# An infini-attention and GeGLU kernel on one core: the recall's copy and sums, the first differences of x, the loads of x's words and four sums of squares change their places

## The chip, the cores and the metric

The kernel runs on one core of a Trainium2 chip. The metric is the device time of one execution in microseconds (us). A core has five engines that run side by side and are tied together by semaphores: TensorE (PE, matmuls, with its weight loads listed as PEld), VectorE (DVE), ScalarE (ACT), GpSimd (POOL) and SyncE (SP, which here only issues DMAs). Matmul results land in PSUM, in eight banks of 128 partitions by 512 fp32 columns.

## The reference

For 2048 tokens of width 576 two branches are computed from the same x and mixed by a gate per token.

```python
def _A_ref(x, wq, wk, wv, wo, beta):          # 32 heads of 18, 4 segments of 512 tokens
    q, k, v = heads of x @ wq, x @ wk, x @ wv
    phi = lambda t: jnp.where(t > 0, t + 1.0, jnp.exp(t))
    M = z = 0
    for s in range(4):
        a_dot = causal softmax attention inside the segment
        num = phi(qs) @ M
        den = phi(qs) @ z + 1e-6
        o = g * num / den + (1.0 - g) * a_dot  # g = sigmoid(beta), per head
        M = M + phi(ks).T @ vs
        z = z + sum over tokens of phi(ks)
    return concat(o) @ wo

def _B_ref(x, w_gate, w_up, w_down):           # 4608 hidden columns
    return (gelu(x @ w_gate) * (x @ w_up)) @ w_down

g = sigmoid((x * gate_w).sum(-1, keepdims=True))
return g * a + (1 - g) * b
```

Everything is fp32 in and out.

## The kernel before

**Pairs of fp16 words.** An fp32 operand is scaled by a power of two and written as two fp16 words, high and low. A product of two such operands is three fp16 matmuls (high by high, high by low, low by high). The scales come from sums of squares, which is what `squares`, `stat_qk`, `square_x` and `scale_sum` compute.

**The part ahead of the long loop.** x is cut into four chunks `s` of 512 tokens, one per segment. Each chunk goes through two stages, written out in the loop from line 797 on:

- rows (`for q in range(4)`, not for chunk 0, whose rows are computed at the start in fp32 by `first_words`): `vrows` makes 128 tokens of v in two halves, `put_rows` evicts them; `key_rows` turns phi(k) of the chunk before with five transposes on PE, `memorize` adds phi(k)ᵀv to the memory, `recall` multiplies phi(q) of the chunk before with the memory, and `put_recall` divides by the sum and writes `mo` out to DRAM;
- columns (`for j in range(9)`): `project` makes 128 columns of q or k for the chunk's 512 tokens by `chain_w`, fourteen matmuls into one bank, and `put_columns` evicts them as word pairs (`stage`, three buffers, to DRAM) and as phi (Relu and Exp on ACT, a multiply on DVE, an addition on POOL).

The recall of chunk 1 runs in the rows of chunk 2, that of chunk 2 in the rows of chunk 3, and that of chunk 3 in the last columns of chunk 3 and after them.

**put_recall, lines 546 to 567.** A recall fills two banks, `na` with heads 0 to 20 and a part of head 21, `nb` with the rest. ACT copies the 19 columns of head 21 from `na` to the tile `hd` (L551), DVE adds them to `nb` (L552), adds 1e-6 to the 32 sums into the tile `den` (L556), takes reciprocals (L559), multiplies by the gate (L560) and writes the quotients (L563), after which the banks are free. `key_rows` of the next step takes one of them (L573).

**x's words and differences.** The FFN's products are arranged with sums and differences of operands, so that fewer products are needed. `load_sums(p)` loads the fp32 words of two chunks into the tile `acc` (L355; `acc` also holds the raw weights wv, wq and wk while these are being converted), `form_sums(p, i, half)` forms difference `i` of three on DVE (L366), its high word on ACT (L368) and its low word on DVE (L370), as `half` says; `last_sum` forms a fourth. The `words` in `kept` are `acc` seen flat.

**Order.** Inside `tc.manual_schedule` each of PE, ACT, DVE and POOL runs its instructions in the order in which the program calls them. A function such as `put_recall` is often appended to the list `later` and runs, on all engines, when `finish_later` is next called. `beside_rows`, `behind_rows` and `beside_products` are the places in a row or column where other work is put: loads of the next chunk (`next_x`), the differences, and, in chunk 3, the first FFN weights with their sums of squares (`squares`, by default on DVE at L81). SP's issues are in no such list: a planner orders them by when their operands are ready in its own model, and SP then issues in that order.

**The long loop.** From line 1383 on, 72 steps make the FFN's products, with the attention of one head and the output products of the pair before between them. The first step's products take the banks V, G and U.

Of the kernel before, what the change touches and what calls it, by code (L numbers as in the profile page):

```python
# [18 lines left out]
P = 128  # L19
# [23 lines left out]
def kernel(ctx: ExitStack, tc: tile.TileContext, xs, wqk, wv, wo, wgu, wd, beta, out):  # L43
# [279 lines left out]
    def chain_w(o, w, x):  # L323

        n = 0
        for k in range(4):
            for a, b in ((0, 0), (0, 1), (1, 0)):
                pe.matmul(o, w(k, a), x[:, 4 * b + k], start=n == 0, stop=False)  # L328
                n += 1
        pe.matmul(o, w(4, 0), x[:, 8], start=False, stop=False)  # L330
        pe.matmul(o, w(4, 1), x[:, 8], start=False, stop=True)
# [26 lines left out]
    def form_sums(p, i, half):  # L358

        r, sc = sums_x[p], xsc[:, 2 * p : 2 * p + 1]  # L360
        t = kept["xt"][p] if half >= 0 else None
        k, o, a, b = ((0, (1, 1), (1, 2), (1, 1)), (2, (1, 2), (2, 2), (1, 2)), (1, (2, 2), (2, 2), (1, 1)))[i]
        if t is not None:
            hi, lo = (flat(t[:, 4 * k + j : 4 * k + j + 2]) for j in (0, 2))
        if half <= 0:
            dve.tensor_tensor(r[o], r[a], r[b], OP.subtract)  # L366
        if half == 0 or half == 2:
            act.activation(hi, r[o], AF.Copy, scale=sc)  # L368
        if half == 1:
            dve.scalar_tensor_tensor(lo, r[o], sc, hi, OP.mult, OP.subtract)  # L370
# [35 lines left out]
    with tc.tile_pool(name="prj", bufs=2, side="right", reuse_waits="tile") as pp:  # L406
# [61 lines left out]
        def project(s, j):  # L468
            w = W[j]
            i = j % 4  # L470
            pr = bank("G") if i == 0 else bank("U") if i == 3 else bank("st", 2)
            chain_w(pr, lambda k, a: w[:, a, k * P : (k + 1) * P], x16[s])
            return s, j, pr
# [72 lines left out]
        def put_recall(s, q, na, nb):  # L546
            hf, c = divmod(s, 2)
            t = 4 * c + q
            dn = pp.tile([P, H], F32, name="den", bufs=2)
            hd = pp.tile([P, MC], F32, name="hd", bufs=2)  # L550
            act.activation(hd, na[:, HS * MC : (HS + 1) * MC], AF.Copy)  # L551
            dve.tensor_tensor(nb[:, :MC], nb[:, :MC], hd, OP.add)  # L552
            o3s = [(slice(0, HS), na[:, : HS * MC].rearrange("p (h d) -> p h d", d=MC)),
# [5 lines left out]
            dve.reciprocal(rd, dn)  # L559
            dve.tensor_tensor(rd, rd, gh[:, 0], OP.mult)  # L560
# [47 lines left out]
        with tc.manual_schedule(engines=ORDERED):  # L608
# [58 lines left out]
            for qs in ((0, 1), (2, 3)):  # L667
                for k in range(0 if qs[0] else 1, KT):
# [3 lines left out]
                    if qs[0] and k == 2:  # L672
                        turns.update(of=2)
                        scale_sum(0, wst[:, 10:19])
                        turns.update(of=3)
                        later.pop(2)()
                        make_qk(0)
                        put_rows(0, 1, 1, vb[1], usc, 1.0)
                        low_x(0, 2)
                        make_qk(1, pair_high)  # L680
                        outscale(0, 0)
                        act.activation(gh[:, 1], gh[:, 0], AF.Exp, scale=-1.0)
# [27 lines left out]
            def beside_rows(s, q):  # L710
                if s == 1 and q == 0:
                    load_sums(0)
                if s == 1 and q == 2:
                    rescale(0)
                    rescale_words(0)
                if s == 2:
                    if q:
                        form_sums(0, q - 1, 1)
                    if q < 3:
                        form_sums(0, q, 0)  # L720
# [10 lines left out]
            def behind_rows(s, q):  # L731
                if s == 3:
                    if q < 3:
                        form_sums(1, q, -1)
# [7 lines left out]
            def beside_products(s, j):  # L742
# [10 lines left out]
                if s < 3:  # L753
                    next_x(s + 1, j)
                if s == 2:
# [4 lines left out]
                    if j == 3:  # L760
                        load_sums(1)
# [3 lines left out]
                if s == 3:  # L765
# [17 lines left out]
                    if j == 7:  # L783
                        squares(1, 3, 0)
                        squares(1, 0, 2)
                    if j == 8:
                        high_g(1, 1)
                        low_g(1, 1)
                        squares(1, 3, 1)
                        squares(1, 1, 2)  # L790
# [53 lines left out]
            put_columns(*done)  # L844
            recall(3, 3)
# [674 lines left out]
```

## Time and profile before

| | us |
|---|---|
| median of 3 runs (lowest to highest) | 1585.94 (1585.93 to 1586.18) |
| the profiled execution | 1585.91 |
| its span, first to last instruction | 1584.2 |
| PE busy | 1569.1 |
| POOL, ACT, DVE busy | 1199.8, 1173.6, 1141.2 |
| DMA moved | 209.00 MB |

The granted TensorE clock was 1.00 throughout. The profile has several views: the page (busy time of each engine, the chain that ended last, the costliest groups), the busy time by stage, the timeline of one engine (start, length, line, operation, and in brackets the idle time in front with what ended it), and the instructions of one line. L551 is line 551 of the kernel before.

### The profile page before, as it was taken

How to read it: one execution, taken by the hardware profiler on the slowest of the kernel's cores; microseconds unless marked ns; L12 is line 12 of the kernel's file. 1: busy time of each engine (PE TensorE's matmuls, PEld its weight loads, DVE VectorE, ACT ScalarE, POOL GpSimd, SP SyncE). 2: the span in 40 equal slices, each digit the busy share in tenths (PEclk: the TensorE clock that was granted, in tenths of full speed). 3: DMA queues.
4: the chain of work that ended last, by engine and by line, in shares of the span. 5: the costliest groups of instructions: out<-in, count | busy, mean ns of one | idle time of the engine just before them, and what ended most of it. 6: DMA issues, size and time to landing. Idle time of an engine off the chain costs nothing.

```text
span 1584.2 us, 32578 instructions
## 1 busy us (share of the span) xinstructions
PE 1569.1 (99%) x11842; PEld 925.7 (58%) x11842; DVE 1141.2 (72%) x2982; ACT 1173.6 (74%) x1989; POOL 1199.8 (76%) x1155
## 2 busy tenths in 40 slices
PE   9999999999999999999999999999999999999999
PEld 5655754555555555555555555555555555555577
DVE  6666786777777677777677777677777777776766
ACT  6665546988888887989888888878798888874310
POOL 2232657798978888887979788888879797887774
PEclk9999999999999999999999999999999999999999
DMA  6532444877799897979788987979797979746163
GB/s 244 196 109 79 148 145 88 139 133 131 128 131 139 128 141 122 145 120 152 136 136 129 130 145 123 154 117 144 120 161 133 139 130 135 132 73 143 38 143 98
DMA packets 472305, 209.00 MB, mean 132 GB/s; under 512 B 427600, under 2 KB 437072, under 8 KB 471632
## 3 DMA queue, kind: packets, MB, share of 16 engines
q1 hardware_dynamic: 472144, 206.92, 72.1%
q8 instruction: 93, 1.52, 0.4%
q14 instruction: 68, 0.56, 0.1%
HBM read 90.99 MB, written 27.26 MB: 75 GB/s over the span
## 4 chain that ended last, share of the span: by engine, by line
PE 96%; DVE 2%; ACT 1%; issue 1%; DMA 0%; POOL 0%; DVEq 0%; ACTq 0%; POOLq 0%
PE dn L1010 26%; PE U L1050 18%; PE V L1050 12%; PE G L1050 12%; PE pv L964 4%; PE U L1056 2%; PE st L328 2%; PE G L328 2%; PE dn L338 1%; PE G L1061 1%; PE V L1061 1%; PE st L914 1%; PE U L1400 1%; PE V L1056 1%; PE G L1056 1%; PE U L328 1%
## 5 line engine op out<-in xcount | busy, mean ns | idle before, releaser
L1010 PE MATMUL dn<-paird,hh 128*128 128x288 f16 x3408 | 485.8, 286 | 0.0
L944 POOL TENSOR_TENSOR ph<-pf,ph 128x512 f16<-128x512 f32 (+1 forms) x256 | 354.2, 1406 | 165.8 <-ACT ph L943 162.8
L1050 PEld LDWEIGHTS <-pairg 128*128 128x128 f16 x3024 | 274.9, 98 | 284.9 <-issue 38.2
L1010 PEld LDWEIGHTS <-hh 128*128 128x128 f16 x3456 | 337.7, 98 | 155.8 <-issue 0.2
L1018 DVE SCALAR_TENSOR_TENSOR acc<-dn,ev,acc 128x288 f32<-128x288 f32 x536 | 275.1, 514 | 65.9 <-PE dn L1010 65.3
L933 ACT ACTIVATE pf<-pf,mb,esc 128x512 f32<-128x512 f32 (+3 forms) x512 | 292.9, 642 | 7.0 <-ACT mb L930 0.4
L1050 PE MATMUL G<-x,pairg 128*128 128x512 f16 x864 | 221.8, 380 | 1.4 <-DVE stage L490 1.3
L1050 PE MATMUL U<-xt,pairg 128*128 128x512 f16 x864 | 210.0, 379 | 0.0
L309 POOL TENSOR_TENSOR pairg<-raw,pairg 128x640 f16<-128x640 f32 (+2 forms) x144 | 175.9, 1245 | 10.5 <-ACT pairg L305 10.5
L1037 POOL TENSOR_TENSOR hh<-gl,hh 128x512 f16<-128x512 f32 x144 | 164.0, 1160 | 16.4 <-ACT hh L1036 16.4
L943 ACT ACTIVATE ph<-pf 128x512 f16<-128x512 f32 (+1 forms) x256 | 172.4, 720 | 0.0
L305 ACT ACTIVATE pairg<-raw 128x640 f16<-128x640 f32 (+2 forms) x144 | 89.9, 651 | 103.8 <-POOL raw L299 53.3
L1215 DVE COPY gl<-U 128x512 f32<-128x512 f32 x72 | 49.8, 692 | 162.0 <-PE U L1050 148.8
L920 DVE CUSTOM_DVE_ANT_0 pf<-st,mask 128x512 f32<-128x512 f32 (+1 forms) x256 | 157.0, 614 | 0.0
L274 POOL TENSOR_SCALAR raw<-raw,sc 128x640 f32<-128x640 f32 x72 | 134.9, 1887 | 0.0
L1040 ACT ACTIVATE gl<-gl,sc 128x512 f32<-128x512 f32 x144 | 96.5, 715 | 41.7 <-DVE gl L1246 28.0
L1050 PE MATMUL U<-x,pairg 128*128 128x512 f16 x432 | 126.9, 378 | 0.4 <-DVE gl L1242 0.4
L920 DVE CUSTOM_DVE_ANT_0 pf<-dn,mask 128x256 f32<-128x256 f32 (+1 forms) x256 | 80.7, 353 | 59.4 <-PE dn L914 59.4
L1036 ACT ACTIVATE hh<-gl 128x512 f16<-128x512 f32 x144 | 85.7, 619 | 28.5 <-DVE gl L1032 28.3
L1050 PE MATMUL V<-xt,pairg 128*128 128x512 f16 x432 | 105.7, 381 | 0.0
L1050 PE MATMUL V<-x,pairg 128*128 128x512 f16 x432 | 104.8, 378 | 0.9 <-DVE gl L1162 0.9
L964 PEld LDWEIGHTS <-pt 128*128 128x128 f16 x2560 | 83.2, 96 | 6.3
(295 smaller groups left out, 2590.1 us busy)
## 6 DMA issues: line engine op xcount, KB each, us to landing
raw<-in_wgu_dram SPq DMA_DIRECT2D x36, 640.0 KB
rawd<-in_wd_dram SPq DMA_DIRECT2D x36, 288.0 KB
qk<-stage SPq DMA_DIRECT2D x36, 256.0 KB
qt<-qk SPq DMA_DIRECT2D x128, 72.0 KB
kt<-qk SPq DMA_DIRECT2D x128, 72.0 KB
vp<-vstage SPq DMA_DIRECT2D x16, 296.0 KB
vt<-vp SPq DMA_DIRECT2D x16, 296.0 KB
qt<-qk SPq DMA_DIRECT2D x128, 36.0 KB
```

The costliest lines, as they stand in the source:

```text
L274: pool.tensor_scalar(r, r, scl[f // 2][0][:, 0:1], None, OP.mult)
L309: pool.tensor_tensor(spot(f, *p, 1), raw_g[f][:, p[0] : p[1]], spot(f, *p, 0), OP.subtract)
L920: dve.tensor_tensor_reduce(prob[a][:, COL[qi] : COL[qi + 1]], ov, mask[:, L - (qi + 1) * P :], 1.0, -3e38, OP.add, OP.max, mx[a][:, qi : q ...
L933: act.activation(r, r, AF.Exp, bias=b[:, qi : qi + 1], scale=esc[:, 0, c : c + 1])
L943: act.activation(h[:, 0, cols], p[:, cols], AF.Copy)
L944: pool.tensor_tensor(h[:, 1, cols], p[:, cols], h[:, 0, cols], OP.subtract)
L964: pe.matmul(ov, pr[:, 10 * i + COL[qi] // P + kb], v[:, 4 * e + kb, c0 : c0 + VC], start=kb == 0 and i == 0, stop=kb == qi and i == 1)
L1010: pe.matmul(o[:, :NH], hh[:, a, q * P : (q + 1) * P], w[:, b, n * NH : (n + 1) * NH], start=i == 0, stop=i == 5)
L1018: dve.scalar_tensor_tensor(av, o[:, :NH], ev, av, OP.mult, OP.add)
L1037: pool.tensor_tensor(hh[:, 1], t, hh[:, 0], OP.subtract)
L1040: act.activation(t, o, AF.Gelu_apprx_tanh, scale=scl[f // 2][0][:, 2 + c : 3 + c])
L1050: pe.matmul(o, w[:, i, (a + k) * P : (a + k + 1) * P], x[:, b + k], start=start and n == 0, stop=n == 5, skip_group_check=True)
```

## The change

1. In `chain_w` an option issues the eight matmuls with the weights' high word first and the four with their low word behind them. It is used for the first column tile of chunk 0 alone. Its weights' high words are made by two ACT instructions in place of one.
2. The loads of x's words for both halves (four DMAs of 1 MB) are called together in the first row of chunk 1. In front of them POOL sets one column of each of the four destinations to zero.
3. The first difference of each half (`form_sums(p, 0, -1)`) moves from the rows of chunk 2, and from behind the rows of chunk 3, to column 3 of chunks 1 and 2. Its high word stays where it was.
4. In `put_recall` the copy of head 21's columns goes from ACT to DVE, and the 32 sums and their reciprocals are kept in free columns of `na`'s bank in place of the tile `den`.
5. Four sums of squares of chunk 3's last columns (two halves of `raw_g[3]`, both `raw_d`) go from DVE to ACT (`act_square`), the last of them behind the last column's eviction.

```diff
-    def chain_w(o, w, x):
-        n = 0
-        for k in range(4):
-            for a, b in ((0, 0), (0, 1), (1, 0)):
-                pe.matmul(o, w(k, a), x[:, 4 * b + k], start=n == 0, stop=False)
-                n += 1
+    def chain_w(o, w, x, low_last=False):
+        words = [(k, a, b) for k in range(4) for a, b in ((0, 0), (0, 1), (1, 0))]
+        if low_last:
+            words.sort(key=lambda i: i[1])
+        for n, (k, a, b) in enumerate(words):
+            pe.matmul(o, w(k, a), x[:, 4 * b + k], start=n == 0, stop=False)
...
-            chain_w(pr, lambda k, a: w[:, a, k * P : (k + 1) * P], x16[s])
+            chain_w(pr, lambda k, a: w[:, a, k * P : (k + 1) * P], x16[s], s == j == 0)
...
-            dn = pp.tile([P, H], F32, name="den", bufs=2)
             hd = pp.tile([P, MC], F32, name="hd", bufs=2)
-            act.activation(hd, na[:, HS * MC : (HS + 1) * MC], AF.Copy)
+            dve.tensor_copy(hd, na[:, HS * MC : (HS + 1) * MC])
             dve.tensor_tensor(nb[:, :MC], nb[:, :MC], hd, OP.add)
+            dn = na[:, 448 : 448 + H]
...
-            dve.reciprocal(rd, dn)
-            dve.tensor_tensor(rd, rd, gh[:, 0], OP.mult)
+            dve.reciprocal(dn, dn)
+            dve.tensor_tensor(rd, dn, gh[:, 0], OP.mult)
...
-                        make_qk(0)
+                        w0 = W[0] = pp.tile([P, 2, KT * P], F16, name="wp", bufs=9)
+                        for cols in (slice(0, 2 * P), slice(2 * P, KT * P)):
+                            act.activation(w0[:, 0, cols], raw_qk[:, 0, cols], AF.Copy, scale=wsc[:, 0:1])
+                        pair_low(w0, raw_qk[:, 0], wsc[:, 0:1])
...
                 if s == 1 and q == 0:
+                    pool.memset(kept["words"][:, 2 * L : 18 * L].rearrange("p (a b) -> p a b", a=4)[:, :, 0:1], 0.0)
                     load_sums(0)
+                    load_sums(1)
...
                     if q < 3:
-                        form_sums(0, q, 0)
+                        form_sums(0, q, 0 if q else 2)
...
                 if s == 3:
-                    if q < 3:
+                    if 1 <= q < 3:
                         form_sums(1, q, -1)
...
+                if s in (1, 2) and j == 3:
+                    form_sums(s - 1, 0, -1)
...
-                    if j == 3:
-                        load_sums(1)
...
                     if j == 7:
-                        squares(1, 3, 0)
-                        squares(1, 0, 2)
+                        squares(1, 3, 0, act_square)
+                        squares(1, 0, 2, act_square)
                     if j == 8:
                         high_g(1, 1)
                         low_g(1, 1)
-                        squares(1, 3, 1)
-                        squares(1, 1, 2)
+                        squares(1, 3, 1, act_square)
...
             put_columns(*done)
+            squares(1, 1, 2, act_square)
             recall(3, 3)
```

More of the change, by code (lines that the diff above doesn't have):

```diff
@@ L360, in form_sums @@
         r, sc = sums_x[p], xsc[:, 2 * p : 2 * p + 1]
-        t = kept["xt"][p] if half >= 0 else None
+        t = kept["xt"][p] if half > -1 else None
         k, o, a, b = ((0, (1, 1), (1, 2), (1, 1)), (2, (1, 2), (2, 2), (1, 2)), (1, (2, 2), (2, 2), (1, 1)))[i]
```

## The prediction

> **What bounds the kernel now.** I read the page first, then the busy time by stage, then PE's timeline wherever a stage is not full.
>
> ```profile
> span 1584.2 us, 32578 instructions
> PE 1569.1 (99%) x11842; PEld 925.7 (58%) x11842; DVE 1141.2 (72%) x2982; ACT 1173.6 (74%) x1989; POOL 1199.8 (76%) x1155
> ...
> 100.00:136.00 36.00, 31.07 (x229) 24.30 (x228) 26.96 (x55) 17.97 (x41) 7.65 (x13) 1.00 0.34 120
> 164.00:192.00 28.00, 26.26 (x211) 22.49 (x209) 20.69 (x61) 11.36 (x31) 17.53 (x20) 1.00 0.37 132
> 205.00:231.00 26.00, 23.75 (x127) 13.58 (x126) 25.13 (x53) 11.06 (x20) 13.96 (x12) 1.00 0.40 142
> 300.00:400.00 100.00, 100.00 (x812) 58.23 (x810) 74.14 (x214) 84.58 (x143) 86.37 (x82) 1.00 0.76 132
> ```
>
> The columns after the length are PE, PEld, DVE, ACT, POOL, clock, DMA share and GB/s. TensorE is the bound: in the long loop (last row) it is busy all the time at clock 1.00, and the whole span has only 1584.2 - 1569.1 = 15.1 us without it. Most of those lie ahead of the long loop, in the three first stages above (4.9, 1.7 and 2.3 us). No edit touches a matmul's size or number, so the change can only win or lose such gaps. These are the gaps, by PE's timeline:
>
> ```profile
> 26.35 2.33 PE L328 MATMUL G<-x,wp 128*128 128x512 f16 x10 [0.32 <-DVE wp L109]
> 56.22 0.30 PE L340 MATMUL dn<-wv,x 128*128 128x288 f16 x1 [0.38 <-DVE x L184]
> 60.80 0.33 PE L574 MATMUL V<-ident,phi 128*128 128x128 f32 x1 [0.28 <-POOL phi L489]
> 112.73 0.63 PE L573 MATMUL st<-ident,phi 128*128 128x128 f32 x4 [1.87 <-DVE mo L563]
> 127.73 0.63 PE L573 MATMUL st<-ident,phi 128*128 128x128 f32 x4 [1.59 <-DVE mo L563]
> 134.22 0.63 PE L573 MATMUL st<-ident,phi 128*128 128x128 f32 x4 [1.47 <-DVE mo L563]
> 171.39 0.63 PE L573 MATMUL st<-ident,phi 128*128 128x128 f32 x4 [0.58 <-ACT vstage L508]
> 190.74 0.63 PE L573 MATMUL st<-ident,phi 128*128 128x128 f32 x4 [1.16 <-DVE mo L563]
> 224.61 1.46 PE L1050 MATMUL V<-xt,pairg 128*128 128x512 f16 x6
> 227.40 1.46 PE L1050 MATMUL G<-x,pairg 128*128 128x512 f16 x6 [1.34 <-DVE stage L490]
> 229.77 1.45 PE L1050 MATMUL V<-x,pairg 128*128 128x512 f16 x6 [0.91 <-DVE gl L1162]
> 234.81 1.29 PE U L1050 x6
> ```
>
> A bracket counts from the drawn end of the last matmul, which overlaps its successor. Measured by starts, G began 2.79 us after V where a group of six takes 1.29 (last row, from the chain), so 1.50 were lost against a bracket of 1.34; the next gap is 2.37 - 1.29 = 1.08 against 0.91. I add 0.15 us to each bracket that disappears.
>
> **The rows of chunks 2 and 3 (put_recall, form_sums).** Five gaps end at key_rows (L573), which needs the PSUM bank that put_recall drains. Why that drain is late:
>
> ```profile
> 106.05 1.37 PE L542 MATMUL st<-bd,phi 128*128 128x152 f32 x10
> 107.00 2.01 DVE L366 TENSOR_TENSOR acc<-acc 128x1024 f32<-128x1024 f32 x1
> 108.93 0.45 DVE L513 SCALAR_TENSOR_TENSOR vstage<-dn,vstage 128x288 f16<-128x288 f32 x1
> 109.05 1.15 ACT L368 ACTIVATE xt<-acc,xsc 128x1024 f16<-128x1024 f32 x1 [1.99 <-DVE acc L366]
> 110.77 0.19 ACT L551 ACTIVATE hd<-st 128x19 f32<-128x19 f32 x1
> 110.99 0.19 DVE L552 TENSOR_TENSOR st<-st,hd 128x19 f32<-128x19 f32 x1 [1.61 <-ACT hd L551]
> ...
> 128.30 1.50 PE L542 MATMUL st<-bd,phi 128*128 128x152 f32 x10
> ...
> 125.12 1.87 DVE L560 TENSOR_TENSOR rden<-rden,gh 128x32 f32<-128x32 f32 x1
> 124.61 2.35 POOL L375 TENSOR_TENSOR acc<-acc 128x1024 f32<-128x1024 f32 x1
> ```
>
> The recall's matmuls end at 107.4, but hd, a copy of 19 columns, stands on ACT behind the wide L368, which waits for DVE's first difference, and behind two evictions. DVE then sits idle for ACT. From L552's start to PE's release are 112.73 - 110.99 = 1.74 us. Now the copy is DVE's own. No row has a DVE copy of this size. It lies between nothing and the 0.19 us of L552, which reads the same 19 columns of PSUM; I take 0.19, and ACT's L551 goes in exchange. With L366 gone from that place, DVE is free at 107.0, does one L513 (0.45), and from 107.5 the copy and the drain take 1.93: released at 109.4, while PE arrives at 110.9. In the last row of the chunk the recall ends at 129.8 and the drain would be over near 132, just ahead of PE's arrival at 134.22 - 1.47 = 132.75. The middle gap also holds L560's 1.87 behind POOL's 2.35; its product now takes a PSUM operand. Even if it still waited for POOL, a row in the middle has one more half of vrows than the last row's 132.75 - 129.8 = 2.95 us between the recall's end and PE's arrival. So all three gaps go: 1.87 + 1.59 + 1.47 = **4.93**.
>
> In chunk 3 the same two causes (a difference of 1.2 us taken out ahead of the first recall, no hd on ACT in the last) take away 0.58 + 1.16 = **1.74**. The last row is the tight one: rescale_words stands on DVE before the drain.
>
> The reciprocal and the product now read dn in PSUM, and L556 writes it there. Nearest are L552 and L556, which read PSUM already; unknown is only the surplus, between a gain of the 1.87's excess and a loss of some 0.1 us a drain; I take none.
>
> [...]
>
> **The moved differences.** They run at column 3 of chunks 1 and 2. Their cover:
>
> ```profile
> 92.44 0.69 DVE L161 TENSOR_REDUCE x<-dn 128x1 f32<-128x512 f32 x1 [4.30 <-PE dn L159]
> L366 DVE TENSOR_TENSOR acc<-acc x6: 1215/1276/2006, 107.0 to 179.1; 128x1024 f32<-128x1024 f32 x6
> ```
>
> L366 took 1.2 to 2.0 us (shortest, median, longest in the row, in ns); in chunk 1 an idle time of 4.3 us stands behind it, and chunk 2 runs the same columns. Cost nothing; uncovered, one would cost its 1.2 to 2.0 us.
>
> **The words of x.** All four loads of 1 MB now wait for a memset of four columns on POOL, in chunk 1's first row, at about 60.8 us.
>
> ```profile
> 34.31 0.33 SPq L355 DMA_DIRECT2D acc<-in_xs_dram  x1
> 51.67 5.59 DMA qk<-stage
> 57.37 0.60 ACT L478 ACTIVATE stage<-G 128x512 f16<-128x512 f32 x1 [1.29 <-DMA qk<-stage]
> 50.00:61.00 11.00, 10.34 (x69) 6.45 (x67) 9.61 (x14) 7.47 (x16) 5.33 (x9) 1.00 0.90 333
> 61.00:82.00 21.00, 21.00 (x154) 16.18 (x153) 7.67 (x23) 8.93 (x23) 2.05 (x7) 1.00 0.23 84
> ```
>
> Those loads (the first of four is shown) filled the DMA engines while the column stages were written out, so ACT waited 1.29 us for a stage buffer, POOL's phi was late by it, and PE lost the **0.28** at 60.80. That goes. The four megabytes now fall into a stretch that moved 84 GB/s: at 333 GB/s 4.2 MB take 12.6 us and the stretch's own 1.8 MB another 5.3, so all is there near 79, ahead of the idle stretch of DVE (88.1 to 92.4) that could still take the first difference. The memset itself lies between nothing and the 2.35 us of a POOL instruction over 1024 columns; I take nothing, since POOL was busy 2 of 21 us there.
>
> **The first column.**
>
> ```profile
> 24.55 0.83 ACT L106 ACTIVATE wp<-acc,wsc 128x640 f16<-128x640 f32 x1 [2.36 <-DVE wsc L93]
> 25.41 0.89 DVE L109 SCALAR_TENSOR_TENSOR wp<-acc,wsc,wp 128x640 f16<-128x640 f32 x1 [0.35 <-ACT wp L106]
> ```
>
> With the high words first, PE no longer waits 0.32 for L109. But two ACT instructions cost one fixed part more (between nothing and 0.2 us; I take 0.12), L109 and all of DVE behind it move by that, the next column waits for its own low word on the same DVE queue, and the 0.38 at 56.22 hangs on DVE and ACT, not on PE. What PE gains it waits for later. I put **0**, between a gain of 0.5 and a loss of 0.2.
>
> **The end of the projections.**
>
> ```profile
> L81 DVE CUSTOM_DVE_ANT_0 junk<-raw x5: 810/1410/1807, 168.9 to 220.9; 128x640 bf16<-128x640 f32 x5
> L81 DVE CUSTOM_DVE_ANT_0 junk<-rawd x2: 1344/1465/1586, 214.8 to 222.8; 128x576 bf16<-128x576 f32 x2
> 167.23 0.72 ACT L437 ACTIVATE krow<-raw 128x640 bf16<-128x640 f32 x1
> 223.60 0.60 ACT L478 ACTIVATE stage<-G 128x512 f16<-128x512 f32 x1 [0.58 <-PE G L331]
> ```
>
> DVE was 25.1 of 26 us busy there, and PE's first FFN products waited for its queue. Four sums of squares leave it (two of 640 columns and two of 576: 2 x 1.41 + 2 x 1.47 = 5.8 us); the four copies return 0.8. ACT has them for about 0.7 us each and was busy 11 of 26 us; the last one stands behind L478, the eviction that PE's G bank needs. L478 ends at 224.2, L490, as wide, can follow by 224.8, ahead of 224.61 + 1.29 = 225.9, when V's group ends. Behind it the last drain takes until 224.8 + 1.93 = 226.7 and L1162, as wide again, until 227.4 or so, where PE wants V at 225.9 + 1.29 = 227.2. Of 1.34 + 0.91 = 2.25 I keep 0.35 as a new wait: **1.9**.
>
> **Sum.** 4.93 + 1.74 + 0.28 + 1.9 = 8.85, plus 0.15 for most of the eight gaps (five counted, since small waits on the transposes' eviction will come back as rows close up), 0.75: 9.6 us. The profiled execution took 1585.91 us, its span and 1.7 around it, beside a median of 1585.94. **1585.9 - 9.6 = 1576.3.**
>
> **Rivals.** (1) DVE becomes the bound of the rows: it now carries the copy, the drain, a difference and a low word each row, by my sum 1.93 + 2 x 0.45 + 1.2 + 1.2 = 5.2 us, where PE takes (127.73 - 1.59 - 112.73) / 2 = 6.7; were the chain late in every second row, 3.3 us would be given back: 1579.6. Against it, the drain starts at the recall's end. (2) The end is not won: ACT's squares are placed ahead of the last eviction, and G is freed 0.7 to 1.4 us late; 1.9 go and up to 0.7 more: 1578.2 to 1579. (3) Slower: SP issues in order. If the loads of words are put ahead of the stage writes of column 5 and later, all of those sit behind a wait for the memset at 60.8, three stage buffers run out, and ACT's L478 at 57.37 waits until 60.8 plus the 5.59 us that such a write took. That is about 9 us for this column and 3 more for each column earlier: 1585 for one, 1588 for two, slower than before from the second on, so from where the first load stands two writes ahead. Before, SP's order followed readiness, which speaks against it. (4) No change: the loop gives the time back. Its PE is full at clock 1.00, so only a late POOL or load at its start could do that: 1584. (5) The memset holds no load back: 0.28 less, inside the range.
>
> **How the numbers follow.** Forecast 0.66, (1) 0.15, (2) 0.08, (4) 0.06, (3) 0.05. Low end: 8.92 + 0.28 and 1.2 by starts, with the first column's 0.7, 11.1 us: 1574.8. The high end takes in (1), (2) and the unknown costs: 1581.0. What this kernel can tell from no change is about 0.2%, 3.2 us: faster 0.89, same 0.06, slower 0.05.
>
> **What would show it.** Right: no gap ahead of L573; the drain on DVE begins at the recall's end; no ACT instruction of 19 columns; the L355 issues after 60 us and the first L366 before 92 without a wait; L490 of the last column ahead of 225. Wrong: L366 waiting for a DMA, SP's stage writes queued behind L355, DVE without idle time in the rows, or PE gaps past 230 us that were not there.

## The result and the profile after

| | before | after |
|---|---|---|
| median of 4 runs each (lowest to highest), us | 1585.99 (1585.93 to 1586.18) | 1576.43 (1576.23 to 1576.74) |
| the profiled execution, us | 1585.91 | 1576.48 |
| span, us | 1584.2 | 1574.8 |

The ratio of the times is 0.994, with a 95% interval of 0.9922 to 0.9957. The kernel became 9.6 us faster, and the prediction was 1576.3.

The page of the kernel after, its first lines, and then the busy time by stage (length, PE, PEld, DVE, ACT, POOL, clock, DMA share, GB/s) for the rows of chunk 2 and the end of the projections:

```profile
span 1574.8 us, 32583 instructions
PE 1568.7 (100%) x11842; PEld 926.2 (59%) x11842; DVE 1138.9 (72%) x2986; ACT 1175.2 (75%) x1986; POOL 1196.1 (76%) x1156
...
100.00:131.00 31.00, 30.83 (x230) 24.39 (x229) 26.92 (x57) 17.84 (x38) 7.92 (x13) 1.00 0.41 145
200.00:222.00 22.00, 22.00 (x121) 12.92 (x120) 19.57 (x48) 12.11 (x22) 11.86 (x12) 1.00 0.44 150
```

PE's busy time is what it was (1568.7 against 1569.1), and the span without PE shrank from 15.1 to 6.1 us. The two stages shown had 4.9 and 2.3 us of idle PE (36 and 26 us long then) and have 0.17 and 0. So nothing became cheaper on PE; waits went away.

A bracket counts from drawn ends, so the account is made from the starts of the same matmuls in both traces. PE's timeline, first of before (rows that the prediction doesn't have), then of after:

```profile
20.23 3.20 PE L533 MATMUL st<-acc,raw 128*128 128x290 f32 x12
62.44 0.29 PE L340 MATMUL dn<-wv,x 128*128 128x290 f16 x1
105.80 0.29 PE L340 MATMUL dn<-wv,x 128*128 128x288 f16 x1
165.75 0.29 PE L340 MATMUL dn<-wv,x 128*128 128x288 f16 x1
231.49 1.46 PE L1050 MATMUL U<-xt,pairg 128*128 128x512 f16 x6
```

```profile
20.89 3.20 PE L533 MATMUL st<-acc,raw 128*128 128x290 f32 x12
57.04 0.30 PE L340 MATMUL dn<-wv,x 128*128 128x288 f16 x1 [0.69 <-DVE x L184]
62.77 0.29 PE L340 MATMUL dn<-wv,x 128*128 128x290 f16 x1
106.12 0.29 PE L340 MATMUL dn<-wv,x 128*128 128x288 f16 x1
129.51 0.60 PE L573 MATMUL st<-ident,phi 128*128 128x128 f32 x4
161.01 0.29 PE L340 MATMUL dn<-wv,x 128*128 128x288 f16 x1
217.75 1.46 PE L1055 MATMUL V<-xt,pairg 128*128 128x512 f16 x6
222.07 1.46 PE L1055 MATMUL U<-xt,pairg 128*128 128x512 f16 x6
```

| stretch of PE's timeline | offset at its end, us | won in it, us | predicted with the 0.15 a bracket, us |
|---|---|---|---|
| start and chunk 0, up to 57.04 | +0.82 | -0.82 | 0 |
| first row of chunk 1, up to 62.77 | +0.33 | 0.49 | 0.28 + 0.15 |
| up to the rows of chunk 2 (106.12) | +0.32 | 0.01 | 0 |
| rows of chunk 2, up to 129.51 | -4.71 | 5.03 | 4.93 + 0.45 |
| columns of chunk 2, up to 161.01 | -4.74 | 0.03 | 0 |
| rows and columns of chunk 3, up to 217.75 | -6.86 | 2.12 | 1.74 + 0.30 |
| end of the projections, up to 222.07 | -9.42 | 2.56 | 1.90 + 0.30 |
| all behind it (span) | -9.4 | 0.0 | 0 |

The last column gives 0.15 to each of the eight gaps and makes 10.05; the prediction counted five of them and said 9.6. The loop neither gave anything back nor won anything.

What the drain of the recall looks like now, on DVE of the kernel after, in the first row of chunk 2 (start, length, instruction; its first and its last):

```profile
107.79 0.17 DVE L550 COPY hd<-st 128x19 f32<-128x19 f32 x1
...
109.21 0.82 DVE L563 TENSOR_TENSOR mo<-st,rden 128x378 f32<-128x378 f32 x2
```

It begins at 107.79, where before the same place held an idle wait until 110.99, and is over at 110.03, one microsecond ahead of PE, which starts its transposes at 111.02. (The change renumbers some lines: L328 of before is L329 of after, L551 is L550, L1050 is L1055 and L1162 is L1167.)

### The profile page after: what moved, and what is told of

Read it like the earlier page. It is cut to its first block, busy times and chain, and to the rows that moved or that the text cites. A ratio compares the mean times of both kernels' runs of the same rounds, so it can differ in the third digit from the quotient of the medians.

```text
span 1574.8 us, 32583 instructions
## 1 busy us (share of the span) xinstructions
PE 1568.7 (100%) x11842; PEld 926.2 (59%) x11842; DVE 1138.9 (72%) x2986; ACT 1175.2 (75%) x1986; POOL 1196.1 (76%) x1156
## 4 chain that ended last, share of the span: by engine, by line
PE 97%; ACT 1%; DVE 1%; issue 0%; POOL 0%; DVEq 0%; ACTq 0%; POOLq 0%
PE dn L1015 27%; PE U L1055 18%; PE V L1055 12%; PE G L1055 12%; PE pv L969 4%; PE U L1061 2%; PE st L329 2%; PE dn L338 2%; PE G L329 1%; PE G L1066 1%; PE V L1066 1%; PE st L919 1%; PE U L1405 1%; PE V L1061 1%; PE G L1061 1%; PE U L329 1%
## 5 line engine op out<-in xcount | busy, mean ns | idle before, releaser
L1055 PEld LDWEIGHTS <-pairg 128*128 128x128 f16 x3024 | 274.9, 98 | 282.2 <-issue 33.4
L1055 PE MATMUL G<-x,pairg 128*128 128x512 f16 x864 | 221.8, 380 | 0.0
L1055 PE MATMUL U<-xt,pairg 128*128 128x512 f16 x864 | 210.0, 379 | 0.0
L274 POOL TENSOR_SCALAR raw<-raw,sc 128x640 f32<-128x640 f32 x72 | 134.7, 1884 | 0.0
L1055 PE MATMUL U<-x,pairg 128*128 128x512 f16 x432 | 126.9, 378 | 0.4 <-DVE gl L1247 0.4
L1055 PE MATMUL V<-xt,pairg 128*128 128x512 f16 x432 | 105.7, 381 | 0.0
L1055 PE MATMUL V<-x,pairg 128*128 128x512 f16 x432 | 104.8, 378 | 0.0
L969 PEld LDWEIGHTS <-pt 128*128 128x128 f16 x2560 | 83.2, 96 | 6.3
```

The source lines that it names most:

```text
L274: pool.tensor_scalar(r, r, scl[f // 2][0][:, 0:1], None, OP.mult)
L969: pe.matmul(ov, pr[:, 10 * i + COL[qi] // P + kb], v[:, 4 * e + kb, c0 : c0 + VC], start=kb == 0 and i == 0, stop=kb == qi and i == 1)
L1055: pe.matmul(o, w[:, i, (a + k) * P : (a + k + 1) * P], x[:, b + k], start=start and n == 0, stop=n == 5, skip_group_check=True)
```

## The experiments

"After, with ..." names the kernel after with one edit, "before, with ..." the kernel before with one edit. Every run was timed in five rounds beside the kernel before on the same chip. There the medians of before were 1586.58 us (the first four kernels below), 1586.41 (the squares alone, no memset, the first column, the sums) and 1586.92 (the other four); the kernel after was timed only beside a before of 1585.99. The same kernel's medians thus differ by up to 0.9 us from group to group, and a smaller difference between kernels of different groups is not told apart by the medians alone.

| kernel | median (range), us | ratio to before, 95% |
|---|---|---|
| copy on ACT again | 1581.65 (1581.52 to 1582.05) | 0.9969 (0.9957 to 0.998) |
| differences in the rows again | 1578.14 (1577.92 to 1578.34) | 0.9946 (0.9934 to 0.9959) |
| squares on DVE again | 1578.51 (1578.04 to 1582.31) | 0.9954 (0.9942 to 0.9967) |
| before, with the copy alone | 1580.63 (1579.9 to 1581.14) | 0.9961 (0.9948 to 0.9975) |
| before, with the squares alone | 1584.32 (1583.53 to 1586.51) | 0.9988 (0.9979 to 0.9997) |
| no memset | 1577.39 (1576.5 to 1578.44) | 0.9942 (0.9928 to 0.9956) |
| first column as before | 1576.09 (1575.85 to 1576.33) | 0.9934 (0.9922 to 0.9947) |
| sums in SBUF again | 1576.26 (1576.03 to 1576.84) | 0.9936 (0.9923 to 0.9948) |
| one more difference a row | 1578.55 (1577.91 to 1580.22) | 0.9948 (0.9935 to 0.996) |
| three more a row | 1589.08 (1587.12 to 1592.35) | 1.0012 (1.0003 to 1.0021) |
| last low word sooner | 1575.28 (1574.86 to 1576.16) | 0.9926 (0.9914 to 0.9939) |
| the same, first column as before | 1575.6 (1575.3 to 1575.86) | 0.9928 (0.9915 to 0.994) |

### After, with the copy on ACT again

```diff
-            dve.tensor_copy(hd, na[:, HS * MC : (HS + 1) * MC])
+            act.activation(hd, na[:, HS * MC : (HS + 1) * MC], AF.Copy)
```

> The changed kernel with head 21's copy back on ScalarE, all else kept. My theory (the drain was late because the copy stood in ScalarE's queue behind two evictions): gaps ahead of the transposes come back in the first and the last row of chunk 2 (about 1.1 and 1.6 us) and in the last row of chunk 3 (1.2), none in the middle rows; with 0.15 for each 4.3 us in all, 1580.7 us. Rival (the moved difference and the sums kept in PSUM did it): 1576.4 to 1577.0.

1581.65 us, 5.2 more than after and 0.95 above the expectation. PE's timeline of this kernel (its gaps in the rows), below it ACT's in the last row of chunk 2, and then DVE's multiplication and POOL's work in the third row:

```profile
112.21 0.63 PE L573 MATMUL st<-ident,phi 128*128 128x128 f32 x4 [1.07 <-DVE mo L563]
132.32 0.63 PE L573 MATMUL st<-ident,phi 128*128 128x128 f32 x4 [1.57 <-DVE mo L563]
169.60 0.63 PE L573 MATMUL st<-ident,phi 128*128 128x128 f32 x4 [0.69 <-DVE mo L563]
188.98 0.63 PE L573 MATMUL st<-ident,phi 128*128 128x128 f32 x4 [1.19 <-DVE mo L563]
```

```profile
129.57 0.43 ACT L508 ACTIVATE vstage<-dn 128x288 f16<-128x288 f32 x1 [2.35 <-PE dn L341]
...
130.26 0.19 ACT L550 ACTIVATE hd<-st 128x19 f32<-128x19 f32 x1
```

```profile
124.81 0.19 DVE L560 TENSOR_TENSOR rden<-st,gh 128x32 f32<-128x32 f32 x1
124.09 2.36 POOL L375 TENSOR_TENSOR acc<-acc 128x1024 f32<-128x1024 f32 x1
```

Four gaps are back, 4.52 us, with 0.15 each 5.1. ACT's copy of 19 columns stands behind L508 (and L510), the evictions of the next half of vrows, and these wait for PE, 2.35 us here; DVE's drain then opens at 130.48 after 2.57 us without work. What was dear was the copy's place in ACT's queue and not the copy. The wide L368, which the prediction named first, is not needed for it: in this row none stands ahead. The gap of the third row of chunk 2 (1.59 before) is not back, though the copy is, and though DVE waits 1.61 us for it there as it did before. What differs is the multiplication L560: in the kernel before it took 1.87 us beside POOL's L375, and here, with the sums in PSUM, 0.19 beside the same L375. So this gap hung on that wait as well, and either edit alone closes it. The gap of chunk 3's first row (0.69) was not expected, and it is most of what the expectation missed.

### Before, with the copy on DVE alone

The same line the other way round, in the kernel before.

> The kernel before with nothing changed but head 21's copy on VectorE. My theory: of the gaps in the rows 1.4 + 1.75 + 1.6 us in chunk 2 and 1.3 in the last row of chunk 3 go, the first row of chunk 3 loses 0.2 and the end 0.6: a gain of 5.2 us, 1580.8 us. Rival (the parts work only together): a gain under 2 us, 1584 or more.

1580.63 us: the copy alone brings 5.4 to 6.0 of the 9.6 us, by the median of before that one takes. PE's timeline of this kernel:

```profile
111.60 0.63 PE L573 MATMUL st<-ident,phi 128*128 128x128 f32 x4 [0.44 <-DVE mo L563]
167.25 0.63 PE L573 MATMUL st<-ident,phi 128*128 128x128 f32 x4 [0.82 <-DVE mo L563]
...
222.19 1.45 PE L1050 MATMUL G<-x,pairg 128*128 128x512 f16 x6 [1.49 <-DVE stage L490]
223.98 1.46 PE L1050 MATMUL V<-x,pairg 128*128 128x512 f16 x6 [0.34 <-DVE gl L1162]
```

Of the five gaps ahead of key_rows 1.26 us are left, in the two rows where a first difference stands on DVE ahead of the drain, and both gaps of the end are still there. The second of these shrank from 0.91 to 0.34 by the copy alone.

### After, with the first differences in the rows again

```diff
-                        form_sums(0, q, 0 if q else 2)
+                        form_sums(0, q, 0)
...
-                    if 1 <= q < 3:
+                    if q < 3:
                         form_sums(1, q, -1)
...
-                if s in (1, 2) and j == 3:
-                    form_sums(s - 1, 0, -1)
```

> The changed kernel with the first differences back in and behind the rows of chunks 2 and 3. My theory (a difference ahead of the first drain on VectorE delays it beyond TensorE's arrival): a gap of about 0.8 us in the first row of chunk 2 and 0.9 in the first row of chunk 3, 1.7 us in all, 1578.1 us. Rival (with the copy on VectorE the drain has room enough, the move is worth nothing): 1576.4.

1578.14 us, 1.7 more than after. PE's timeline of this kernel:

```profile
111.84 0.63 PE L573 MATMUL st<-ident,phi 128*128 128x128 f32 x4 [0.54 <-DVE mo L563]
167.60 0.63 PE L573 MATMUL st<-ident,phi 128*128 128x128 f32 x4 [0.93 <-DVE mo L563]
```

The two gaps are the ones that the copy alone leaves, 0.54 + 0.93 + 2 x 0.15 = 1.8. So the first row of either chunk needs both edits: 0.54 and 0.93 are left without the moved difference, 1.07 and 0.69 without the copy. The last rows need the copy alone.

### After, with the squares on DVE again

```diff
-                        squares(1, 3, 0, act_square)
-                        squares(1, 0, 2, act_square)
+                        squares(1, 3, 0)
+                        squares(1, 0, 2)
...
-                        squares(1, 3, 1, act_square)
+                        squares(1, 3, 1)
+                        squares(1, 1, 2)
...
-            squares(1, 1, 2, act_square)
```

> The changed kernel with the four sums of squares back on VectorE. My theory (VectorE's queue set when the banks G and V of the first FFN products came free): the two gaps at the end of the projections come back, 2.6 us, and the copies that VectorE now carries there add up to 0.6: 1579.0 to 1579.6 us. Rival (the end got shorter because the rows in front of it did): 1576.4.

1578.51 us, 2.1 more than after, with runs up to 1582.31; the expectation was 0.5 to 1.1 higher. PE's timeline of this kernel, in an execution of 1580.25 us:

```profile
220.81 1.46 PE L1055 MATMUL G<-x,pairg 128*128 128x512 f16 x6 [1.71 <-DVE stage L490]
```

The wait for G's eviction is back with 1.71. The wait for V is not: here, too, the planner put L1167 ahead of the end of the last drain. In this execution the attention in the loop (L969, at 299.75) also waited 1.67 us for a load, at a place that no edit touches; 1580.25 - 1.67 = 1578.6 lies at the median.

### Before, with the squares on ACT alone

The same edit the other way round, in the kernel before.

> The kernel before with nothing changed but the four sums of squares on ScalarE. My theory: the two gaps at the end of the projections go, 2.3 to 2.6 us, the gaps in the rows stay as they were: 1583.4 to 1583.7 us. Rival (ScalarE's copy of head 21 then stands behind the squares and VectorE waits for it): under 1 us, 1585 or more.

1584.32 us over 11 runs, 1.7 to 2.1 less than before by the median taken; the expectation's 1583.4 to 1583.7 was missed by 0.6. PE's timeline of this kernel, in its slowest execution (1586.51 us):

```profile
63.23 0.33 PE L574 MATMUL V<-ident,phi 128*128 128x128 f32 x1 [1.64 <-POOL phi L489]
...
230.12 1.46 PE L1050 MATMUL V<-x,pairg 128*128 128x512 f16 x6 [0.34 <-DVE gl L1162]
```

G's gap is gone and V's has 0.34 left, of 2.25 in all, as the prediction's sum had it. But the gap for phi, 0.28 in the trace of before, is 1.64 here, and no edit touches that place. That gap is a matter of the execution, as the next experiment shows.

### After, without the memset

```diff
-                    pool.memset(kept["words"][:, 2 * L : 18 * L].rearrange("p (a b) -> p a b", a=4)[:, :, 0:1], 0.0)
```

> The changed kernel without the memset ahead of the loads of x's words; all four loads stay called together. My theory (the memset is what holds the loads back, and without it they share the DMA engines with the stage writes again): loads issued from about 35 us on, ScalarE waits over 1 us for a stage buffer again and TensorE 0.3 to 0.45 us for phi: 1576.7 to 1576.9 us. Rival (the loads' place in the program sets their time): issued at 60 us as before, 1576.4.

1577.39 us, half a microsecond above the expectation; its fastest run is as fast as after, its slowest 2 us slower. What the memset does, by SP's first issue of the words in the kernel after (the others follow by 62.9):

```profile
60.60 0.35 SPq L355 DMA_DIRECT2D acc<-in_xs_dram  x1
```

Without it the planner puts those loads at 34.70 to 49.59, among the stage writes of chunk 0's columns. ACT then waits 2.83 us for a stage buffer in front of column U's eviction, and PE for phi:

```profile
61.57 0.33 PE L574 MATMUL V<-ident,phi 128*128 128x128 f32 x1 [0.68 <-POOL phi L489]
```

The eviction of column U, first in the kernel before, then in the kernel after:

```profile
54.24 0.60 ACT L478 ACTIVATE stage<-U 128x512 f16<-128x512 f32 x1 [2.14 <-DVE phi L488]
```

```profile
52.37 0.57 ACT L478 ACTIVATE stage<-U 128x512 f16<-128x512 f32 x1
```

All four traces without the memset have this wait: 2.14 in before, 2.24 with the copy alone, 2.83 here, 3.58 with the squares alone. In before the profile names a phi on DVE, but after runs the same eviction 1.9 us ahead of that phi (54.29), so it does not hang on it; in the other three the stage write is named. The gap on PE is 0.28, none, 0.68 and 1.64. None of the ten traces with the memset has a wait for U or a gap for phi. The wait in front of G, 1.38 in the kernel after, does not come from those loads: it stands in all of these traces with 1.0 to 1.4, and by itself it doesn't reach PE. By the medians of one chip (1576.09 and 1576.26 for the next two kernels, which keep it) the memset is worth some 1.2 us, more than the 0.43 predicted for it and more than the 0.68 that this trace shows; the spread of the runs without it is 1.9 us, against 0.5 and 0.8 of those two, and its lowest run lies within the range of the second.

### After, with the first column as before

The option of chain_w is not used, and make_qk(0) makes the weights of the first column.

> The changed kernel with the first column as in the kernel before (one wide eviction of its high words, low words in between). My theory (what TensorE wins there it waits for later, at the last low word of x of chunk 1, since VectorE's queue sets that): the 0.3 us gap at the first column comes back, the 0.69 at the last low word becomes 0.4 or less, total unchanged within 0.2 us: 1576.4. Rival (a real gain): 0.3 to 0.5 slower, 1576.8.

1576.09 us, 0.3 less than after, which these runs don't tell from no difference. The wait for L109 is back (0.32), and the gap at L340 falls from 0.69 to 0.37: the edit moves 0.32 us from one gap to the other. A later experiment says which work stands at the second.

### After, with the sums in SBUF again

```diff
-            dn = na[:, 448 : 448 + H]
+            dn = pp.tile([P, H], F32, name="den", bufs=2)
...
-            dve.reciprocal(dn, dn)
-            dve.tensor_tensor(rd, dn, gh[:, 0], OP.mult)
+            dve.reciprocal(rd, dn)
+            dve.tensor_tensor(rd, rd, gh[:, 0], OP.mult)
```

> The changed kernel with the 32 sums and reciprocals in an SBUF tile again, the copy staying on VectorE. My theory: no gap opens, since the drain has over 1 us of room in every row, and only in the very last drain could its length show: within 0.2 us of 1576.4. Rival (keeping them in PSUM is what freed the drain from waiting for GpSimd): a wait of up to 1.9 us at the multiplication in some row and a gap of about 1 us: 1577.4.

1576.26 us, not told from after. The instructions by line (count, busy time, mean in ns, idle before), first of the kernel after (nine of its twelve; the others have other banks), then of this one:

```profile
L559 DVE RECIPROCAL st<-st 128x32 f32<-128x32 f32 x9 | 3.3, 367 | 0.3
L560 DVE TENSOR_TENSOR rden<-st,gh 128x32 f32<-128x32 f32 x9 | 1.7, 191 | 0.3
```

```profile
L559 DVE RECIPROCAL rden<-den 128x32 f32<-128x32 f32 x12 | 4.2, 353 | 0.4
L560 DVE TENSOR_TENSOR rden<-rden,gh 128x32 f32<-128x32 f32 x12 | 3.4, 286 | 0.4
```

From PSUM the reciprocal takes 14 ns more, and the multiplication 95 ns less in the mean, though not in the median (192 ns against 191): with both operands in SBUF the twelve make 3.4 us, where twelve of the median would make 2.3, so some took longer. Writing the sums into PSUM also lengthens the two L556 ahead of them, from 0.29 to 0.39 us together. None of this is on PE's path any more, now that each drain ends ahead of PE.

### How much room DVE has in the rows

In each row of chunk 2 one more difference of 1024 columns on DVE, whose result is not used; in a second kernel three of them, range(3). The expectations below speak of the first three rows, but the loop stands outside `if q < 3`: the traces have 4 and 12 of these instructions, in all four rows.

```diff
                         form_sums(0, q, 0 if q else 2)
+                    for _ in range(1):
+                        dve.tensor_tensor(kept["words"][:, : 2 * L], kept["words"][:, 2 * L : 4 * L], kept["words"][:, 2 * L : 4 * L], OP.subtract)
```

> The changed kernel with one more difference of 1024 columns (its result is not used) on VectorE in each of the first three rows of chunk 2. It asks how near VectorE is to setting the pace of the rows. My theory (5.2 of 6.7 us a row are used, so 1.2 us just fit): a gap of 0.3 us or less in the first row, none in the others, 1576.4 to 1576.8 us. Rival (VectorE is at its limit there): 1.2 us a row, 1580 us.

> The same with three more differences a row, 3.6 us. My theory: the row needs 8.9 us of VectorE against 6.7 of TensorE, so gaps of 2.2 to 2.6 us ahead of the transposes in three rows, 6.5 to 7 us in all, 1583 us. Rival (a drain waits for the recall alone, VectorE's load is hidden): 1576.4.

One more: 1578.55 us, 2.1 more than after, between the two expectations. PE's timeline of that kernel:

```profile
111.04 0.63 PE L573 MATMUL st<-ident,phi 128*128 128x128 f32 x4 [0.55 <-DVE mo L563]
115.55 1.04 PE L585 MATMUL U<-v,krow 128*128 128x152 f32 x6 [0.76 <-DVE vstage L513]
130.92 0.63 PE L573 MATMUL st<-ident,phi 128*128 128x128 f32 x4 [0.42 <-DVE mo L563]
```

1.73 in brackets and 3 x 0.15 make 2.2; the last of the three is in the fourth row. The largest is not where I had looked: memorize (L585) waits for L513, which is queued on DVE behind the differences. Two of the instructions took longer than the sum had them: the added difference of the first row 2.00 us, where the others take 1.21 and 1.22, and L370 in the fourth 2.77, where those of the second and third row take 1.28 and 1.27. The kernel after has an L489 (at 106.98) and the L375 (at 123.10) on POOL at these places.

Three more: 1589.08 us, 12.7 more than after where 6.6 were expected (for three rows). The profiled execution took 1589.72. PE's timeline of that kernel, its gaps, one behind each row's three differences, and one group of a column; then its busy time in two windows (length and PE first; the clock is the third number from the end):

```profile
114.00 1.08 PE L573 MATMUL st<-ident,phi 128*128 128x128 f32 x4 [3.07 <-DVE mo L563]
121.03 1.04 PE L585 MATMUL U<-v,krow 128*128 128x152 f32 x6 [1.76 <-DVE vstage L513]
130.05 1.63 PE L338 MATMUL dn<-wv,x 128*128 128x288 f16 x12 [0.80 <-DVE vstage L513]
139.94 0.63 PE L573 MATMUL st<-ident,phi 128*128 128x128 f32 x4 [2.87 <-DVE mo L563]
140.51 4.44 PE L329 MATMUL G<-x,wp 128*128 128x512 f16 x12
```

```profile
114.00:116.00 2.00, 2.00 (x9) 2.00 (x10) 2.00 (x5) 0.77 (x2) 0.00 (x0) 0.50 0.51 195
...
137.76:141.18 3.42, 1.24 (x9) 0.91 (x10) 2.52 (x11) 0.52 (x2) 0.00 (x0) 1.00 0.08 29
```

The four gaps make 8.5, with 0.15 each 9.1. The rest is the clock. After each of the two long gaps the granted clock was 0.50 (the first window shown lies behind the first; from 142 to 144 it was the same): the transposes of the first row take 1.08 us in place of the 0.60 that the kernel after shows at 129.51, and the same twelve matmuls of L329 that take 2.75 us there take 4.44 here. From 114.00 to 118.86, where the next half of vrows ends its chain, 4.86 us pass where after has 3.57 (111.02 to 114.59): 1.3 lost; L329 loses 1.7. That is 9.1 + 3.0 = 12.1, and the first FFN group of this trace starts 12.15 us later than that of after. So this run is no measure of DVE's load alone: 3.0 us of it are the slow matmuls behind the gaps of 3.07 and 2.87 us.

Read in windows of 0.1 us the clock is at half from 113.87 to 117.28 and from 141.18 to 144.59, 3.41 us each time. From fall to fall are 27.31 us, eight times 3.41. The second fall did not come in the gap: in the 3.42 us ahead of it (second row above) PE was busy for 1.24, from the end of the gap on. The gap of 1.87 in before left the clock at 1.00.

### The wait that was left: the last low word of chunk 1's x

In the kernel after the largest bracket between start and loop is the 0.69 at 57.04, where PE waits for L184, a low word of x, which stands on DVE behind a column's phi and eviction. The edit calls it ahead of them:

```diff
-                if 6 <= j:
+                if 6 <= j < (8 if c == 1 else 9):
                     low_x(c, j - 6)
+                if c == 1 and j == 7:
+                    low_x(c, 2)
```

> The changed kernel with the last low word of x of chunk 1 ahead of one column's eviction on VectorE (column 7 in place of 8). My theory (the gap of 0.69 us in the first row of chunk 1 is VectorE's queue, and it eats what the first column gains): the gap goes, 0.6 to 0.8 us, unless phi of the last column is late by 0.1 or 0.2 in its place: 1575.6 to 1575.9 us. Rival (TensorE then waits the same time for phi): 1576.4.

> The same with the first column as in the kernel before. My theory: with the wait at the last low word gone the first column's gap of 0.3 us is no longer made good later, so this one is 0.1 to 0.4 slower than the run with the first column changed: 1575.9 to 1576.1 us. Rival (the first column's edit costs more on ScalarE and VectorE than it gains on TensorE): as fast or faster, 1575.4 to 1575.6.

1575.28 us and, with the first column as before, 1575.6. DVE's row for L184, of the kernel after and then of the first of these two:

```profile
55.55 1.44 DVE L184 SCALAR_TENSOR_TENSOR x<-raw,xsc,x 64x512 f16<-64x512 f32 x1
```

```profile
54.39 0.73 DVE L184 SCALAR_TENSOR_TENSOR x<-raw,xsc,x 64x512 f16<-64x512 f32 x1
```

It comes 1.16 us sooner and takes half the time, as POOL's phi addition, which runs from 55.17 to 56.43 in the kernel after, is not beside it here (it starts at 55.93); PE's gap at L340 is gone. The version beats both kernels: ratio to before 0.9926 (0.9914 to 0.9939). It is 0.3 below its expectation and 1.15 us below after, with ranges that do not meet (1576.16 at the highest, 1576.23 at the lowest), though the two were not timed on one chip. Whether the first column's edit now pays is not settled: 1575.6 lies below the expectation (1575.9 to 1576.1) and at the edge of its rival, and the ranges of 1575.28 and 1575.6 overlap; the bracket that comes back without it is 0.32.

## Why the prediction was right, and where its sizes were off

**The bound.** PE's time did not change, all of the gain came out of idle brackets, and the loop kept it. That part stands as it was.

**The rows of chunk 2, 4.93 and 0.45 for starts: right, 5.03 by starts.** The cause was ACT's queue, as said: undoing the copy costs 5.2 us, doing it alone wins 5.4 or more. In the first row it took the moved difference as well, and the gap of the third row hung also on L560's wait beside POOL, which the prediction left open: it does not come back with the copy on ACT once the sums are in PSUM. The DVE copy took 0.17 where 0.19 was assumed. From the copy's start to the drain's end 2.24 us pass, not 1.93; it cost nothing, as PE came a microsecond later. The 0.15 for each bracket came back only in part: PE of after still has 0.17 us of small waits in this stage.

**The rows of chunk 3, 1.74: right, 2.12 by starts.** By the two undone kernels its first row needs both edits (0.93 is back without the moved difference, 0.69 without the copy), its last row the copy (1.19). The moved difference of chunk 1 started at 85.10, without a wait, so the words were there.

**The sums in PSUM, no value: right.** From PSUM the reciprocal takes 14 ns more and the multiplication, in the median, 1 ns less. What did lengthen the drain is L556, by 0.10 us for writing into PSUM: the loss of some 0.1 us a drain that the prediction had allowed for. The edit had no value because the copy's move is enough: with the copy on DVE and the sums in SBUF again PE has no wait at L573.

**The end, 1.9: a little too low, 2.56 by starts.** The step that failed is the new wait of 0.35, for L1162 behind the whole last drain. DVE's timeline of after shows the order that the planner chose:

```profile
219.28 0.68 DVE L1167 COPY gl<-V 128x512 f32<-128x512 f32 x1
219.88 0.81 DVE L563 TENSOR_TENSOR mo<-st,rden 128x378 f32<-128x378 f32 x2
```

L1167 (L1162 of before) stands ahead of L563, ends at 219.96, and PE takes V at 220.34 without a wait. With the squares alone, where L1162 stands behind the drain, the new wait is there with 0.34, so the step held for that order and failed by the new one. L490 came at 217.37, which is 224.2 on the clock of before (V starts 6.86 us sooner), ahead of the 225 that was the mark, behind ACT's 0.6 us of L478 as assumed. Rival 2, the squares put ahead of the eviction, did not come.

**phi, 0.28: 0.49 by starts, the mechanism right, the instruction wrong.** The loads did leave the column stages, and with them ACT's 2.14 us in front of U's eviction. The 1.29 us of G's wait, which the prediction named as the cause, is still there with 1.38, so it was not these loads that made it.

**The first column, 0: inside its bounds, but the start was not constant.** Of the +0.82 at 57.04, 0.66 stand already at 20.89, ahead of any instruction that the change touches: the first four fp32 matmuls took 2.25 us in place of 1.54, for a reason that the profile does not name (in five other traces PE waits for a load of wv ahead of a later group of four, 0.23 to 0.71 us). From 20.89 to the end of the first column the edit won 0.67. The two ACT instructions of its high words took 1.01 us together where the one took 0.83: 0.18 more, for which the prediction had taken 0.12. The second column, whose weight loads waited 0.60 us for their own low word (L109), gave back 0.53, and L340 took 0.30 more (its bracket went from 0.38 to 0.69), since the next chunk's low word on DVE was the later wait. Both are what the prediction said; the net is a loss of 0.16.

**The sum.** 9.43 between the two profiled executions and 9.56 between the medians, where 9.6 was said. The nearness is in part luck: the end's 0.36 more and the three brackets that were not given their 0.15 were offset by the start's 0.66 and the 0.16. The 0.35 by which the rows of chunk 2 fell short of the table, half made up by small gains elsewhere, is what is left between 9.43 and 9.6. Two bounds of the prediction were loose: its low end counts 0.7 for the first column, whose gain it had bounded by 0.5, and its high end of 1581.0 and rival 4's 1584 stand without a sum.

**Rival 1, DVE as the bound of the rows: not there, but nearer than summed.** The sum of 5.2 us in 6.7 left 1.5 a row; one more difference of about 1.2 us in each of the four rows already costs 2.1 in all. The sum left out POOL: beside it L370 runs up to 3.4 us and a difference 2.0, where 1.2 was counted for either. **Rival 3** (SP's order) did not come; the loads stand behind the stage writes of columns 5 to 7, and the write of column 8 (61.05) stands behind the first of them. **Rival 4** did not come: the loop gave nothing back. **Rival 5** neither: the memset moved the first load from 34.70 to 60.60.

## What to carry to other kernels

A short instruction costs what stands ahead of it in its queue: a copy of 0.19 us on the wrong engine cost 5 us because evictions that wait for later matmuls stood in front of it. So move the small links of a chain to the engine that does the rest of it. Where an engine sets the end, list its brackets with their releasers, ask of each which instruction of the releaser's queue can go elsewhere, and account for the gain by starts of the same matmuls rather than by brackets. When a wait at the head of a chain is removed, look whether the next one on the same queue was already later, and try a change in the order of that one first.

## What the hardware did that was not expected

- **The clock fell to 0.50 twice, the second time 1.24 us after PE had gone back to work.** The gaps ahead were of 3.07 and 2.87 us, it stayed at 0.50 for 3.41 us each time, and the two falls are eight times 3.41 us apart. Of the 3.42 us ahead of the second 2.18 were idle. In the 3.42 us behind the first return (117.28 to 120.70) 1.42 were idle, of the gap of 1.76 us, and no fall followed. How much idle time a fall takes was not measured. The two falls cost 3.0 us beyond the gaps' own length.
- **Fifteen DVE instructions with two operands in SBUF that began beside a two-operand instruction of POOL ended after it, by 0.03 to 1.09 us.** The timelines of DVE and POOL in the kernel after:

```profile
123.10 3.43 DVE L370 SCALAR_TENSOR_TENSOR xt<-acc,xsc,xt 128x1024 f16<-128x1024 f32 x1
123.10 2.36 POOL L375 TENSOR_TENSOR acc<-acc 128x1024 f32<-128x1024 f32 x1
```

The shortest of the six L370 takes 1.27 us; this one takes as long as POOL's instruction and 1.07 more, as if it had been held until POOL was done. Thirteen more instructions of this trace with two tensors in SBUF (L179, L184, L366, L370) began while a POOL L489 ran: the ten of 1024 columns ended 1.08 or 1.09 us after it, the three of 512 columns 0.55 or 0.56. L560 with SBUF operands (32 columns, 1.87 us in before) ended 0.03 after POOL's L375; with one operand in PSUM it took 0.19 beside the same L375. Beside POOL's L274, a TENSOR_SCALAR, one L366 took 1.78 us and ended with it, so this is no rule for every POOL instruction. That the whole instruction is held and not slowed is the author's reading of these ends; no run here was made to show it, or its cause.

- **Waits for DMA differed from trace to trace.** In the four traces without the memset ACT's wait for a stage write at one place of the program is 2.1 to 3.6 us, which cost PE 0 to 1.64, and a load in the loop gave PE 1.67 us once. How much of the spread between runs of one kernel this makes was not shown.
